# Phase-mixing kernel behind local attention: q and k of the last batch transposed by DMA, another order of the first loads, shallower load gates

## The chip, the cores and the metric

The kernel runs on one core of one Trainium2 chip. The metric is the device time of one execution in microseconds (us); less is better. The kernel before takes 171.01 us, the median of three runs (170.99 to 171.37).

## What is computed

Four batches, eight heads, 768 positions, head size 64; the model width is 8 x 64 = 512. First comes attention with a linear bias, where a position sees itself and the 95 positions before it (n_local = 96) and the first 8 positions (n_global = 8):

```python
scores = scale * q @ k.T + bias          # bias = -slope[h] * distance
scores = where(is_global | is_local, scores, -1e9)
a = exp(scores - max); a = a / (sum(a) + 1e-9)
x = (a @ v)  ->  [batch, 768, 512]
```

Then a block that mixes positions and channels:

```python
theta = x @ w_theta
zr, zi = x * cos(theta), x * sin(theta)
y = w_tok_r @ zr + w_tok_i @ zi          # over positions, per batch
u = x + y
out = u + max(u @ w_ch, 0)
```

## The kernel before

**Tiling.** The 768 positions are six tiles of 128. Two tiles make a "third", so a batch `b` has thirds `g` = 0, 1, 2. The 8 heads are four pairs `p`, since two heads of 64 fill 128 partitions.

**Operations and their names.** Each step is recorded by `add` under a name, and a list written out by hand, `ORDER`, says in which order the steps are issued. Each engine works off its own steps in that order, and waits where an operand or a buffer isn't ready. So the list sets the order on every engine, the DMA queues included. The names that matter here (digits are batch, third, and so on; a trailing `/DVE` or `/ACT` chooses the engine):

- `hw..`, `cast..`: q and k of the first third of batch 0 are loaded as float32 by plain DMAs on SP and ACT, and cast to bf16 (L293).
- `load<n>`: the n-th load on the queue of GpSimd (POOL), which casts from float32 to bf16 on the way: `load_qk` (L247), `load_v` (L261), `load_w` (L267), `load_w_tok` (L273). Their order is the order of the calls from L300 on; for the first loads the branch `ORD` chooses it.
- `gate<n>`: a copy of one element on POOL (L234) that reads what load n - depth has brought. It is issued just ahead of load n, so POOL can't issue load n until the earlier one has landed. The depth is 8 for batch 1 and `DEPTH` for batches 2 and 3.
- `t<b><g><i><u>`: the transpose of q (i = 0) or k (i = 1) of a third, to put the head size on partitions: eight 128x128 transposes on TensorE into PSUM (L425; L418 in the first third). `q...` and `k...` copy them out of PSUM (L439, L436). `kp` and `kg` (L384, L388) make a second copy of k whose first 8 columns are those of the global positions.
- `vpa`, `vpb` (L457, L460): the same second copy for v.
- `bi` (L490): a matmul that puts the bias into PSUM (batch 0 only). `s` (L499): scores. `x` (L526): exponential on ACT. `m` (L534): multiplication by `etab`, the exponential of the bias (L742), for batches 1 to 3. `v` (L556): values. `n` (L567, L569): the division by the sum.
- `xt` (L582 on TensorE with the copy `xc`; for batches 2 and 3 a DMA transpose on SP, L589): x transposed. `th` (L601): theta. `ts`, `tx`: loading of ACT's tables for sine and exponential (L733, L713). `cos`, `sin` (L610, L612), `z` (L622).
- `tw`, `twc` (L367, L372): the token weights transposed. `mx` (L644): the mixing over positions. `u` (L656). `ut`: u transposed, by DMA on SP (L676) or TensorE (L668, with the copy `uc`). `ch` (L688), `o` (L694), `st` (the store on SP, L704).

A name with `+n` asks for n fill matmuls on zeros ahead of its own (`fill`, L142 to 147), 128 columns wide into a bf16 tile (L145), else as wide as the tile (L147). The figures that are given to `add` for each engine (`{"DVE": 0.34}`) are estimates from which an order was once planned; when the kernel runs, only the first key of such an entry is used, as the engine where the list names none.

PSUM has two pools of four buffers, `pa` (scores, theta, values) and `pb` (the rest). A scores step takes two `pa` buffers, which the exponentials free; a theta takes one, which its sine frees.

Of the kernel before, what the change touches and what calls it, by code (L numbers as in the profile page):

```python
# [15 lines left out]
class Plan:  # L16
# [6 lines left out]
    def add(self, name, eng, fn, **_):  # L23
        op = self.ops[name] = SimpleNamespace(name=name, fn=fn, took=next(iter(eng)))
        return op
# [12 lines left out]
zero hw00 hw10 halfpi rel ones2 ones1 hw01 warm0 ones0 hw11 ones5 ones3 ones6 ones4 load1 tiny sid4 sid3 sid7  # L38
sid1 sid0 sid2 load2 sid5 sid6 ident far0 far1 load3 dtab0 dtab1 dtab2 load4 cast00/ACT dtab3 bi0000+1
cast10/DVE etab5 bi0001 t0000 load5 t0010 q000/ACT bi0010 bi0011 k000/DVE load6 etab7 kg000 cast01/DVE etab4  # L40
load7 kp000/DVE t0001+22 cast11/DVE etab1 s001 q001/DVE t0011 load8 etab0 s000 k001/DVE x0000 load9 kg001
x0001 kp001/DVE t0100+14 etab6 bi0020 load10 bi0021 q010/DVE x0010 t0110 x0011 s002 load11 k010/DVE etab2
bi0030 bi0031 s003 kp010/DVE x0020 load12 x0021 vpa00/DVE bi0100+2 x0030 kg010 vpb00/DVE bi0101+1 load13 x0031
s010 etab3 v000 v002 load14 v001 n000 x0100 bi0110 bi0111 vpa01/DVE s011 x0101 load15 vpb01/DVE bi0120 x0110
v003 n002 bi0121 load16 s012 x0111 n003 bi0130 load17 x0120 v010 n001 bi0131 s013 x0121 load18 n010 bi0200
x0130 v012 load19 v011 x0131 n012 t0200 gate20 t0210 n011 q020/ACT load20 v013 k020/DVE xt00 gate21 bi0201
kg020 xc00/ACT bi0210 kp020/DVE load21 bi0211 vpa02/DVE s020+1 n013 s021 gate22 x0200 vpb02/DVE load22 xt01+6
x0201 bi0220 x0210 xc01/DVE v020+1 bi0221 x0211 gate23 n020 bi0230 load23 s022 bi0231 x0220 s023 gate24 tw00
x0230 load24 th001 twc00/DVE x0231 gate25 x0221 v021 load25 v023 n021 ts0 tw10 gate26 v022 load26 twc10/DVE
th000 n023 gate27 tw11 n022 cos000 load27 th010 twc11/DVE sin000 xt02 gate28 cos001 z000 load28 tw01 sin001  # L50
th011 xc02/DVE gate29 cos010 z001 load29 th020 sin010 twc01/DVE gate30 cos011 load30 th021 z010 sin011 gate31
cos020 t1000 load31 z011 tw20 sin020 q100/DVE tw21 cos021 gate32 mx000 z020 load32 twc20/ACT twc21/DVE mx001
gate33 sin021 vpa10/DVE load33 tx1 vpb10/DVE t1010 z021 mx020 gate34 k100/DVE load34 mx002 kp100/DVE gate35
kg100 mx022 load35 u00 gate36 s100 load36 s101 ut00 x1000 mx021 gate37 x1010 uc00/DVE load37 x1001 tw31 x1011
u02 tw30 twc31/ACT gate38 s102 m100 load38 s103 t1100 x1020 m101 x1030 mx010 gate39 q110/DVE x1031 load39
x1021 v100 m103 mx012 twc30/ACT m102 gate40 load40 n100 tw40 v102 twc40/DVE mx011 gate41 n102 load41 t1110 u01
tw41 gate42 v103 k110/DVE load42 twc41/ACT ut01 ut02 v101 kg110 uc02/DVE ch00 uc01/ACT gate43 kp110/DVE load43
vpa11/DVE ch01 n103 gate44 load44 vpb11/DVE s110 n101 t1200 gate45 x1100 o00 load45 ch02 x1101 q120/DVE st00
t1210 gate46 o01 load46 s111 k120/DVE s112 st01 x1110 mx030 gate47 kp120/DVE x1120 load47 o02 mx032 x1121
kg120 gate48 x1111 m110 st02 mx031 load48 m111 s113 gate49 u03 s120 load49 x1130 tw50 m112 tw51 twc50/ACT v110  # L60
gate50 twc51/DVE xt10 load50 x1131 n110 mx040 vpa12/ACT xc10/DVE gate51 mx042 load51 m113 x1200 mx041
vpb12/DVE x1201 gate52 load52 m120 v111 mx050 n111 gate53 load53 u04 s121 v120 x1210 v113 gate54 n120 ut03
load54 x1211 mx052 n113 uc03/ACT gate55 m121 mx051 load55 vpa20/DVE s122 u05 gate56 s123 x1220 ch03 load56
vpb20/DVE x1221 ut04 x1230 gate57 o03 ut05 v121 load57 uc04/ACT v112 n121 th100 st03 uc05/ACT gate58 n112
x1231 load58 ch04 m122 ts1 m123 gate59 xt11 load59 v122 xc11/DVE cos100 v123 th101 gate60 n122 sin100 load60
n123 ch05 cos101 o04 gate61 sin101 xt12 load61 o05 st04 th110 xc12/ACT vpa21/DVE gate62 st05 z100 th111 load62
cos110 z101 sin110 th120 gate63 vpb21/DVE load63 cos111 z110 th121 sin111 gate64 cos120 load64 t2110 z111
sin120 t2010 k210/DVE gate65 cos121 t2200 load65 z120 mx100 k200/ACT kp210/DVE gate66 q220/DVE mx101 sin121
load66 kp200/DVE tx2 t2000 z121 gate67 mx120 kg210 load67 vpa22/DVE q200/DVE mx102 gate68 vpb22/DVE load68
kg200 mx110 u10 gate69 s200 load69 ut10 s201 mx111 x2000 x2001 gate70 x2010 mx121 load70 m200 x2011 v200 m201  # L70
gate71 mx112 load71 n200 s202 u11 gate72 s203 t2100 x2020 load72 x2021 mx122 ut11 q210/DVE x2030 gate73 x2031
m202 t2210 load73 u12 s210 k220/ACT s211 gate74 vpa30/DVE ut12 ch10 load74 vpb30/DVE x2100 kp220/DVE x2101
mx130 gate75 o10 load75 x2110 m210 s212 x2111 st10 mx131 gate76 m203 x2120 load76 m211 x2121 v210 mx132 n210
gate77 load77 m212 v201 s213 n201 ch11 gate78 x2130 load78 kg220 u13 x2131 v202 s220 n202 gate79 ut13 v203
load79 mx140 x2200 m213 x2201 n203 s221 gate80 load80 v212 vpa31/DVE x2210 xt20 mx142 m220 x2211 gate81 n212
s222 load81 v220 vpb31/DVE x2220 v213 n220 mx141 gate82 x2221 load82 n213 v211 m222 s223 ch12 n211 x2230 x2231
m221 v222 xt21 mx150 ts2 m223 v221 n222 v223 mx151 n221 n223 th200 o12 xt22 th201 o11 cos200 vpa32/DVE sin200
mx152 st11 u14 cos201 st12 vpb32/DVE ch13 sin201 ut14 u15 z200 th210 ut15 o13 th211 cos210 z201 sin210 st13
th221 cos211 z210 t3000 sin211 t3010 q300/DVE t3110 k300/DVE t3210 th220 k310/DVE k320/ACT kp300/DVE t3100
z211 cos220 mx200 kg300 q310/DVE sin220 mx201 cos221 kg310 kp310/DVE kg320 sin221 kp320/DVE t3200 z220 tx3  # L80
ch15 q320/DVE z221 s300 s301 mx220 x3000 o15 x3001 x3010 mx202 st15 m300 x3011 s302 m301 s303 mx222 u20 x3020
x3021 x3030 ut20 v300 m302 mx221 x3031 n300 v302 m303 ch14 n302 s310 o14 s311 x3100 mx210 u22 st14 x3110 v303
x3111 ut22 mx212 n303 x3101 m311 mx211 m310 v301 ch20 u21 n301 ut21 mx230 o20 s312 st20 s313 x3120 mx232 xt30
x3130 v310 x3121 ch22 n310 x3131 m312 s320 s321 o22 x3200 mx250 x3201 m313 st22 v311 x3210 mx231 n311 x3211
m320 s322 s323 u23 x3220 mx251 x3221 m321 ut23 v313 x3230 ch21 m322 x3231 n313 ts3 v312 v321 m323 mx240 n312
v320 o21 v322 xt31 mx241 n320 n321 v323 mx242 st21 n323 n322 th300 u24 xt32 mx252 cos300 sin300 th301 u25 ut24
z300 ch23 cos301 ut25 sin301 th310 o23 z301 th311 st23 cos310 sin310 mx300 cos311 z310 th320 sin311 z311 th321
cos320 sin320 mx301 cos321 z320 ch24 sin321 z321 mx310 o24 mx302 st24 mx311 u30 mx312 ut30 ch25 u31 mx320 ut31
o25 mx322 st25 mx321 ch30 u32 mx330 ut32 o30 mx331 st30 mx332 ch31 u33 mx340 ut33 o31 mx342 st31 mx341 ch32
u34 mx350 ut34 o32 mx351 st32 mx352 ch33 u35 ut35 o33 ch34 uc35/ACT st33 ch35 o34 ch351 o35 st34 o351 st35  # L90
st351
# [4 lines left out]
def kernel(  # L96
# [13 lines left out]
    nc = tc.nc  # L110
# [18 lines left out]
    add = plan.add  # L129
# [33 lines left out]
    TQ = ()  # L163
    TQ_AFTER = None
    DEPTH = 6
# [37 lines left out]
    add("dtab0", {"DVE": 0.34},  # L203
        lambda: nc.vector.tensor_tensor(dtab[:, 0:2], rel, far, op=ALU.add),
        reads=["far"], writes=["dtab"], prio=-6)
    add("dtab1", {"DVE": 0.11}, lambda: nc.vector.tensor_copy(out=dtab[:, 2], in_=dtab[:, 0]),
        reads=["dtab"], writes=["dtab"], prio=-6)
    add("dtab2", {"DVE": 0.14},
        lambda: nc.vector.tensor_scalar(dtab[0:NG, 0:2], dtab[0:NG, 0:2], float(NL), None, op0=ALU.min),
        reads=["dtab"], writes=["dtab"], prio=-6)  # L210
    add("dtab3", {"DVE": 0.14}, lambda: nc.vector.tensor_copy(out=dtab[:, 3:5], in_=dtab[:, 1:3]),
# [66 lines left out]
    def first(i, t):  # L278
# [18 lines left out]
        o = add(f"cast{i}{t}", {"DVE": 0.34, "ACT": 0.49}, cast, reads=[st], writes=[key, key + (i, t)],  # L297
# [10 lines left out]
    ORD = 2  # L308
# [66 lines left out]
    def twin(dst, mine, b, g, u0, n):  # L375
# [5 lines left out]

        def copy():
            d_ = tiles[dst][:, :, pr] if halves else tiles[dst][:, u0:u0 + n]
            vector[oc.took](out=d_[:, :, :, 1, NG:T], in_=d_[:, :, :, 0, NG:T])  # L384

        oc = add(f"kp{b}{g}{u0}", {"DVE": dve_t(512 * n, 4), "ACT": act_t(512 * n)}, copy, reads=mine, writes=[dst] + w2)
        add(f"kg{b}{g}{u0}", {"DVE": 0.1},
            lambda: nc.vector.tensor_copy(  # L388
                out=tiles[dst][:, td, kd, 1, 0:NG],
                in_=tiles["kk", b, 0][:, 0:1, kd, 0, 0:NG].to_broadcast([T, td.stop - td.start, kd.stop - kd.start, NG])),  # L390
            reads=mine + first_k, writes=[dst] + w2, boost=boost(b, 3))

    def trans_qk(b, g, i, ts):
# [404 lines left out]
```

The softmax here doesn't subtract the row's maximum and nothing guards it: scores larger than these inputs give would overflow.

## Time and profile before

| what | value |
|---|---|
| median of the runs | 171.01 us (170.99 to 171.37) |
| the profiled execution | 171.41 us |
| its span, first to last instruction | 169.6 us |
| TensorE (PE) busy | 162.1 us, 96% |
| VectorE (DVE) busy | 136.0 us, 80% |
| ScalarE (ACT) busy | 103.9 us, 61% |
| GpSimd (POOL) busy | 80.7 us, 48% |
| q and k transposes on PE (L425) | 176 |
| fill matmuls on PE (L145; L147) | 42; 6 |

The profile is that of one execution. Its time is the span and 1.8 us around it. "PE" is TensorE, whose matmuls overlap: the duration of one is longer than the step from one to the next, so costs are read from the chain of waits, where a run of matmuls is given as start, length and count. That chain is followed back from the last instruction, at each step to what released it. Views of waits give the total in us, the times and the longest. A window's row gives start and end, its length, then busy us and instructions of PE, the weight load of PE, DVE, ACT and POOL, the granted clock, the DMA share and GB/s. A row of DMA issues gives the transfer, the queue, the number, the size, and the median us from issue to landing.

### The profile page before, as it was taken

The numbers are of one execution on the slowest core, as the hardware profiler recorded it, in microseconds if no ns is written. First come the engines' busy times: TensorE is split into PE (matmuls) and PEld (weight loads), VectorE is DVE, ScalarE is ACT, GpSimd is POOL, SyncE is SP. The second block draws the span as 40 slices with busy tenths as digits, with TensorE's granted clock in tenths as the row PEclk, the third lists the DMA queues.
The fourth block names the chain that finished last, engine by engine and source line by source line (L and its number), as shares of the span: only waits on it lengthen the run. The fifth ranks groups of instructions, "written<-read, shape, count | busy, mean of one in ns | idle before, by whom it ended". The sixth has DMA issues, their size and how long they took to land.

```text
span 169.6 us, 4122 instructions
## 1 busy us (share of the span) xinstructions
PE 162.1 (96%) x1581; PEld 91.9 (54%) x1608; DVE 136.0 (80%) x316; ACT 103.9 (61%) x186; POOL 80.7 (48%) x150
## 2 busy tenths in 40 slices
PE   7999999999999999999999999999999999999990
PEld 2665756656655656565555554754545644444440
DVE  7888987896999999998699999898859965634442
ACT  3799989986454939994695666695448557200010
POOL 8998689969989989999950000000000000000000
PEclk9999999999999999999999999999999999999999
DMA  4999999999999999999999438303363373143334
GB/s 134 208 155 155 197 191 177 190 178 178 162 164 197 197 143 137 164 221 141 135 156 139 93 66 216 93 0 97 93 126 98 74 173 97 62 108 108 95 97 182
DMA packets 94820, 23.73 MB, mean 140 GB/s; under 512 B 86992, under 2 KB 91856, under 8 KB 94800
## 3 DMA queue, kind: packets, MB, share of 16 engines
q0 software_dynamic: 73504, 12.33, 96.4%
q1 hardware_dynamic: 20240, 10.62, 23.4%
q10 hardware_dynamic: 1056, 0.52, 1.2%
q8 instruction: 12, 0.20, 0.5%
q14 instruction: 8, 0.07, 0.1%
HBM read 25.69 MB, written 6.29 MB: 189 GB/s over the span
## 4 chain that ended last, share of the span: by engine, by line
PE 87%; DVE 6%; ACT 2%; issue 2%; DVEq 0%
PE pb L644 37%; PE pa L601 12%; PE pb L688 10%; PE pa L499 7%; PE pb L425 5%; PE pa L556 5%; PE pa L490 3%; PE pb L367 2%; PE pb L582 2%; PE pb L556 2%; ACT e L526 1%; PE pb L668 1%; DVE sid L215 1%; ACT etab L742 1%; DVE kk L384 1%
## 5 line engine op out<-in xcount | busy, mean ns | idle before, releaser
L644 PE MATMUL pb<-zri,w_tokT 128*128 128x512 bf16 x273 | 67.6, 379 | 1.0 <-issue 0.3
L526 ACT ACTIVATE e<-pa 128x512 bf16<-128x512 f32 (+1 forms) x96 | 47.2, 568 | 25.1 <-PE pa L499 25.0
L644 PEld LDWEIGHTS <-w_tokT 128*128 128x128 bf16 x288 | 25.9, 98 | 26.7
L656 DVE TENSOR_TENSOR u<-x,pb 128x512 bf16<-128x512 bf16 x24 | 16.4, 683 | 11.1 <-PE pb L644 11.1
L534 DVE TENSOR_TENSOR e<-e,etab 128x1024 bf16<-128x1024 bf16 (+1 forms) x36 | 22.3, 639 | 2.6 <-ACT e L526 2.4
L688 PE MATMUL pb<-w_ch_bf,uT 128*128 128x512 bf16 (+1 forms) x96 | 24.0, 371 | 0.2
L601 PE MATMUL pa<-w_theta_bf,xT 128*128 128x512 bf16 x90 | 22.5, 379 | 0.3
L610 ACT ACTIVATE cs<-pa,halfpi 128x512 bf16<-128x512 f32 x24 | 16.8, 700 | 7.9 <-PE pa L601 7.8
L261 POOL DMA_DIRECT2D vn<-in_v_dram x24 | 21.2, 892 | 0.6 <-DMA qk<-in_q_dram 0.4
L247 POOL DMA_DIRECT2D qk<-in_q_dram x22 | 19.6, 890 | 1.4 <-issue 0.7
L247 POOL DMA_DIRECT2D qk<-in_k_dram x22 | 19.3, 879 | 0.4 <-issue 0.3
L622 DVE TENSOR_TENSOR zri<-x,cs 128x1024 bf16<-128x1024 bf16 x24 | 16.4, 685 | 3.5 <-ACT cs L612 3.5
L556 PEld LDWEIGHTS <-e 128*128 128x128 bf16 x352 | 15.0, 98 | 5.8
L694 DVE SCALAR_TENSOR_TENSOR o<-pb,u 128x512 f32<-128x512 f32 (+1 forms) x25 | 16.3, 663 | 2.3 <-PE pb L688 2.3
L569 DVE TENSOR_TENSOR x<-pa,rec 128x256 bf16<-128x256 f32 x36 | 15.3, 425 | 1.2
L499 PE MATMUL pa<-qT,kk 64*128 64x128 bf16 x352 | 15.9, 218 | 0.3 <-DVE qT L436 0.2
L499 PEld LDWEIGHTS <-kk 64*128 64x128 bf16 x352 | 10.0, 94 | 10.8 <-issue 8.1
L612 ACT ACTIVATE cs<-pa 128x512 bf16<-128x512 f32 x24 | 14.7, 612 | 0.0
L672 ACT COPY uT<-pb 128x512 bf16<-128x512 bf16 x5 | 2.8, 589 | 18.8 <-PE pb L668 18.8
L601 PEld LDWEIGHTS <-xT 128*128 128x128 bf16 x96 | 9.0, 98 | 9.5 <-DVE xT L585 0.2
L688 PEld LDWEIGHTS <-uT 128*128 128x128 bf16 x100 | 8.9, 98 | 8.8 <-ACT uT L672 0.5
L425 PE MATMUL pb<-ident,qk 128*128 128x128 bf16 x176 | 12.5, 219 | 0.1
(76 smaller groups left out, 205.3 us busy)
## 6 DMA issues: line engine op xcount, KB each, us to landing
out_dram<-o SPq DMA_DIRECT2D x23, 256.0 KB, 2.5
vn<-in_v_dram POOLq DMA_DIRECT2D x24, 128.0 KB, 5.6
qk<-in_q_dram POOLq DMA_DIRECT2D x22, 128.0 KB, 5.7
qk<-in_k_dram POOLq DMA_DIRECT2D x22, 128.0 KB, 5.5
w_nat<-in_moe_w_tok_r_dram POOLq DMA_DIRECT2D x6, 192.0 KB, 7.9
w_nat<-in_moe_w_tok_i_dram POOLq DMA_DIRECT2D x6, 192.0 KB, 7.3
e<-in_k_dram ACTq DMA_DIRECT2D x2, 256.0 KB, 5.0
e<-in_q_dram SPq DMA_DIRECT2D x2, 256.0 KB, 4.3
```

The costliest lines, as they stand in the source:

```text
L247: nc.gpsimd.dma_start(out=tiles[key][:, i, t].rearrange("p (h d) -> p h d", d=D), in_=(q, k)[i][b, :, r0:r0 + T, :].rearrange("h p d -> p ...
L261: nc.gpsimd.dma_start(out=v_bufs[i][:, t, :, 0:D], in_=v[b, :, r0:r0 + T, :].rearrange("h p d -> p h d"))
L425: nc.tensor.transpose(p_[:, t - u0, p], tiles[key][:, i, t, p * T:(p + 1) * T], ident)
L499: nc.tensor.matmul(p_[hh][:, s], lhsT=tiles["kk", b, kg][R, kt, p, r, :], rhs=tiles["qT", b, g][R, qt, p, :], start=not biased, stop=not b ...
L526: nc.scalar.activation(tiles[ek][:, hh, 0:n], tiles[pb[hh]][:, 0:n], AF.Exp, scale=scale)
L534: nc.vector.tensor_mul(e_[:, :, 0:n], e_[:, :, 0:n], etab[:, 2 * p:2 * p + 2, s0:s0 + n])
L556: nc.tensor.matmul(o, lhsT=l_, rhs=r_, start=(i == 0), stop=(i == len(mms) - 1))
L601: nc.tensor.matmul(p_, lhsT=tiles["xT", b, g][:, p, t, :], rhs=w_theta_bf[:, p, :], start=(p == 0), stop=(p == NP - 1))
L610: nc.scalar.activation(tiles[ck][:, 0], tiles[ps], AF.Sin, bias=halfpi)
L622: nc.vector.tensor_mul(tiles[zk][:, t].rearrange("n i (p c) -> n i p c", p=NP), tiles["x", b, g][:, None, :, t, :].to_broadcast([T, 2, NP, ...
L644: nc.tensor.matmul(p_, lhsT=w_tokT[wi][:, 2 * g + t, tt * T:(tt + 1) * T], rhs=tiles["z", b, g][:, t, wi, :], start=(n == 1 and t == 0 and ...
L688: nc.tensor.matmul(p_, lhsT=tiles["uT", b, tt][:, p, :], rhs=w_ch_bf[:, p, i * w:(i + 1) * w], start=(p == 0), stop=(p == NP - 1))
```

## The change

The diff, with the list cut to two places:

```diff
-    TQ = ()
+    TQ = ((3, 0), (3, 1), (3, 2))
     TQ_AFTER = None
-    DEPTH = 6
+    DEPTH = 4
...
-    ORD = 2
+    ORD = 5
```

The branches of `ORD` that are concerned, unchanged in both kernels (`third(g)` is q and k of third g of batch 0):

```python
    elif ORD == 2:
        third(1), load_v(0, 0), load_v(0, 1), third(2), load_v(0, 2)
...
    elif ORD == 5:
        third(1), load_v(0, 0), third(2), load_v(0, 1), load_w("w_theta", w_theta_bf, moe_w_theta, 2.4), load_v(0, 2)
    if ORD < 3:
        load_w("w_theta", w_theta_bf, moe_w_theta, 2.4)
```

The branch of `trans_qk` that `TQ` selects, which was in the kernel before but not used:

```python
        if (b, g) in TQ:
            def go():
                ...
                nc.sync.dma_start_transpose(out=d_, in_=tiles[key][:, i].rearrange("n t c -> n (t c)"))
            add(f"t{b}{g}{i}{u0}", {"SP": 1.3}, go, ...)
            if i == 1:
                twin(dst, mine, b, g, u0, n)
            return
```

So for the three thirds of batch 3 six DMA transposes on SP's queue take the place of 48 transposes on TensorE and of the six copies out of PSUM; `kp` and `kg` stay.

The list is new as a whole; all engines get another order. The first lines, before and after, and the passage from batch 2 to batch 3:

```diff
-zero hw00 hw10 halfpi rel ones2 ones1 hw01 warm0 ones0 hw11 ones5 ones3 ones6 ones4 load1 tiny sid4 sid3 sid7
-sid1 sid0 sid2 load2 sid5 sid6 ident far0 far1 load3 dtab0 dtab1 dtab2 load4 cast00/ACT dtab3 bi0000+1
-cast10/DVE etab5 bi0001 t0000 load5 t0010 q000/ACT bi0010 bi0011 k000/DVE load6 etab7 kg000 cast01/DVE etab4
-load7 kp000/DVE t0001+22 cast11/DVE etab1 s001 q001/DVE t0011 load8 etab0 s000 k001/DVE x0000 load9 kg001
-x0001 kp001/DVE t0100+14 etab6 bi0020 load10 bi0021 q010/DVE x0010 t0110 x0011 s002 load11 k010/DVE etab2
...
-th221 cos211 z210 t3000 sin211 t3010 q300/DVE t3110 k300/DVE t3210 th220 k310/DVE k320/ACT kp300/DVE t3100
-z211 cos220 mx200 kg300 q310/DVE sin220 mx201 cos221 kg310 kp310/DVE kg320 sin221 kp320/DVE t3200 z220 tx3
-ch15 q320/DVE z221 s300 s301 mx220 x3000 o15 x3001 x3010 mx202 st15 m300 x3011 s302 m301 s303 mx222 u20 x3020
...
+zero hw00 hw10 ones3 rel ones1 ones2 hw01 warm0 ones0 hw11 ones4 ones5 tiny halfpi load1 ones6 far0 far1 dtab0
+load2 dtab1 dtab2 load3 dtab3 sid2 ident etab3 sid4 sid7 load4 sid5 sid1 cast00/DVE etab4 sid6 load5 sid0
+t0000+11 etab6 cast10/DVE bi0000 bi0001 q000/DVE etab0 t0010 load6 bi0010 k000/DVE cast01/ACT load7 kp000/DVE
+cast11/ACT t0001+18 kg000 sid3 etab2 q001/DVE s000+1 load8 t0011 x0000 bi0011 s001 k001/DVE x0001 load9 bi0020
+t0100 x0010 kg001 etab5 kp001/DVE bi0021 load10 bi0030 q010/DVE t0110 etab1 s002 load11 k010/DVE x0011 x0020
...
+mx150 m222 x2230 ut14 x2231 o11 v221 mx152 ts2 m223 ut13 v222 n221 v223 mx151 n222 t3000 n223 th201 o12 xt22
+th200 vpa32/DVE u15 th211 cos200 t3010 vpb32/DVE sin200 th210 cos201 z200 t3110 ch14 sin201 cos210 z201 ch13
+t3210 sin210 o14 cos211 mx210 o13 sin211 ut15 mx200 z210 z211 t3100 th220 th221 st12 cos220 st14 sin220
+kp300/DVE mx211 st13 kg300 cos221 z220 st11 s300 sin221 mx201 t3200 tx3 z221 s301 kg310 kp310/DVE mx212 x3000
+x3010 mx202 kg320 u21 x3001 x3011 kp320/DVE s302 ut21 u20 s303 ch15 x3020 m301 x3021 x3030 ut20 m300 mx220
```

The fills ("+n") are 22 and 14 ahead of `t0001` and `t0100`, 6 ahead of `xt01`, 1 to 2 ahead of `bi0000`, `bi0100`, `bi0101`, `s020` and `v020` before; after, they are 11 and 18 ahead of `t0000` and `t0001`, 1, 3 and 2 ahead of `s000`, `bi0031` and `bi0210`. The remaining lines of the diff change planned figures of `add` (such as `{"DVE": 0.34}` to `0.4`), which no running instruction uses.

## The prediction

> **What bounds the kernel now.** I read the page's first line, then who TensorE (PE) waits for, then busy time by stretch, then the chain of waits at the two places that the change touches.
>
> ```profile
> PE 162.1 (96%) x1581; PEld 91.9 (54%) x1608; DVE 136.0 (80%) x316; ACT 103.9 (61%) x186; POOL 80.7 (48%) x150
> ```
>
> ```profile
> PE pb L355 <- DVE zero L185: 1.2, 1, 1.2
> PE pb L644 <- issue: 0.3, 2, 0.2
> PE pa L147 <- ACT e L526: 0.2, 1, 0.2
> ```
>
> ```profile
> 0.00:15.00 15.00, 13.03 (x127) 7.58 (x129) 12.51 (x41) 10.61 (x20) 14.22 (x21) 1.00 1.74 165
> ...
> 35.00:105.00 70.00, 69.12 (x727) 40.26 (x739) 63.95 (x148) 47.74 (x86) 49.84 (x94) 1.00 1.75 157
> 105.00:115.00 10.00, 9.95 (x92) 6.00 (x92) 9.14 (x20) 8.22 (x15) 0.00 (x0) 1.00 0.22 58
> ```
>
> PE is busy for 96% of the span, its waits sum to about 2 us, and between 15 and 165 us it is idle for hardly 1%. The granted clock is 1.00 all the way. So past the first 15 us a microsecond of PE work taken away is a microsecond of time, as long as nothing else becomes late; an engine freed elsewhere gives nothing. In the first 15 us a part of "busy" is padding (next part), so there the chain decides, not the busy share.
>
> **Term 1: 48 transposes leave PE.** For batch 3, TQ turns six groups `t3..` of eight 128x128 transposes (L425) into DMA transposes on SP. The chain shows what they hold of PE, pipelined:
>
> ```profile
> 107.16 1.79 PE pb L425 x32
> 108.95 0.86 PE pa L601 x4
> 109.81 0.45 PE pb L425 x8
> ...
> 111.98 0.45 PE pb L425 x8
> ```
>
> 1.79 + 0.45 + 0.45 = **2.69 us** (0.056 us a transpose; the 219 ns of the group's row is one transpose's latency, not its pitch). They are links of the chain themselves, so nothing hides them. Their copies out of PSUM go too: five of 0.69 us on DVE and one of 1.01 us on ACT. These engines are not the bound; I count them at nothing.
>
> What is added is six transposes on SP, of 256 KB each like `xT<-x`:
>
> ```profile
> xT<-x SPq DMA_TRANSPOSE x6, 3.1
> ```
>
> The timeline has 1.24 us of SP for the issue of one, and 3.1 us from issue to landing. First need: `s300` reads k of the first third after `kp300` and `kg300` (0.40 + 0.17 us on DVE). On SP `t3010` stands behind `xt22`, which waits for the last norm `n223`. After `v223` ends, three norms take 3 x 0.55 = 1.65 us, `xt22` 1.25, then 3.1 to 3.4 for `t3010`, and 0.6 for the copies: 6.7 us. On PE, between `v223` and `s300` stand mx151, four thetas, ch14, ch13, mx210, mx200, th220, th221 and mx211: 12 x 0.865 = 10.4 us. Cover left: 3.7 us. Even the 5.4 us that two uT transposes took at 84 to 90 us, beside loads, would fit. `xt22` itself is wanted by th220, eight PE groups (7 us) after `v223`; 1.65 + up to 1.25 for the `t3000` ahead of it + 3.1 = 6.0. Cover 1 us. Behind the six on SP wait `ut15` and four stores; `ut15` is delayed by some 5 us and its user ch15 stands seven PE groups later; the stores' buffers are asked for later still. So the moved work is hidden; without that cover each late transpose would cost its whole lateness.
>
> What becomes tighter is ACT. Before, ACT had slack between the sines of batch 2 and the first exponentials of batch 3, given by these very transposes:
>
> ```profile
> 112.16 1.28 ACT L713 ACT_TABLE_LOAD   x1
> 113.45 0.20 ACT L713 ACTIVATE tiny<-tiny 1x1 f32<-1x1 f32 x1
> 113.60 1.64 ACT L526 ACTIVATE e<-pa 128x384 bf16<-128x384 f32 x4
> ```
>
> After: th220 and th221 stand together, so the second cosine and sine end 0.25 + 1.06 us after th221, the table takes 1.44, and x3001, third in ACT's order, ends 1.25 later: 4.0 us, and about 0.1 for semaphores. PE has in that time mx211, s300, mx201, s301, mx212, mx202 = 4 x 0.865 + 2 x 0.23 = 3.9 us before s302 wants the buffers. Stall 0.2 to 0.3 us; I take **+0.25**, bounds 0 (the thetas start a little earlier) and +1.0 (one more ACT copy of 1.01 us' size in between).
>
> The Trainium skill speaks against this part: "VectorE: DVE Perf Modes", section "Rules for kernel authors", says to transpose 128x128 on TensorE where a PSUM destination will do, and its section "The three transpose paths" gives 390 ns there against 1309 ns by DMA. The trace agrees on the order (0.056 us of PE pitch against 3.1/8 = 0.39 us by DMA). By that rule the part would gain nothing and the whole change about 0.7 us; but the rule prices a transpose alone and not an engine that is full.
>
> **Term 2: start-up and padding.** The new order also has fewer fill matmuls (the "+n"): transposes 42 -> 29, 13 x 0.056 = 0.73 us; wide ones 6 -> 6 with more of the 0.16 kind and fewer of 0.216, 0.17 us; together 0.90 us, of which 0.55 before the first values matmul. A fill only fills a wait: if the wait is there anyway, nothing is won. So the chain must be walked:
>
> ```profile
> 11.89 0.38 ACT e L526
> 12.27 0.62 ACT etab L742
> 12.89 0.39 ACT e L526
> ...
> 13.32 0.38 PE pa L147
> ```
>
> From 10.0 to 13.3 us ACT ends last: eight exponentials of the first third (0.41 each) with three etab (0.62) between. ACT began them at 10.0 since s000 ended there, behind DVE's casts and copies. After: DVE does the far/dtab chain first (from 1.65: 0.45 + 0.41 + 0.45 + 0.32 + 0.25 + 0.62, so dtab ends at 4.15 and not at 5.9; the next starts some 0.3 before that end, as it did before), then six of the sid and ident (0.23 each), cast00 at 5.3, two sid, cast10 to 6.65, q000 and k000 (0.65 each) to 8.0, kp000 and kg000 to 8.6 to 9.0. So s000 ends at 8.9 to 9.4 and ACT starts 0.6 to 1.1 earlier; its five etab and two casts of before that (from 4.15: 5 x 0.65 + 2 x 0.6) end at 8.6 and are no obstacle. DVE's further chain (q001, k001, kp, kg, q010, k010, kp, kg, then vpa00, vpb00) ends at 14.0 to 14.6 against 14.77 before. I take **-0.6**, bounds -1.0 and +0.2 (the slow rows of the same copies: vpa00 took 0.84 and not 0.43). Later pads: 0.35 us fewer; before had no PE wait there, so I take **-0.3**, bounds -0.35 and 0.
>
> Moved loads, in POOL's queue at 0.87 us a place and some 6.9 us to landing: q, k of the last third come two places earlier; v of the middle third four places later, at 17.7 to 18.6 us, and its users moved behind s021 (about 21 us); w_theta two places earlier, at some 20 to 21 us, wanted by th001 at about 23.3; v of the last third at some 22, wanted by v020 at 25. Each has over 1 us of cover: nothing. If the cover of v went, PE would wait by the lateness.
>
> **Term 3: gates four deep, from load 47 on.** A gate on POOL waits until the load four places earlier has landed; behind it on POOL stand all later loads. Six deep, the 36 loads took 40.2 us, 1.12 us each (0.87 issue, 0.18 gate copy, few waits). Four deep the pace is at least (landing + 0.2) / 4. The landing depends on what is under way; two short stretches (47 to 50 us, 50 to 56 us beside stores):
>
> ```profile
> qk<-in_q_dram POOLq DMA_DIRECT2D x2, 128.0 KB, 4.5
> ```
> ```profile
> qk<-in_q_dram POOLq DMA_DIRECT2D x2, 128.0 KB, 6.7
> ```
>
> With 4.5 us the pace is 1.18 and the last v lands at 91.5 + 36 x 0.06 = 94; with the window's median of 5.0 it is 1.30 and 98. Its first user is this DVE copy, which stands in DVE's order ahead of u15 and will come some 3 us sooner:
>
> ```profile
> 102.35 0.43 DVE L457 COPY vp<-vn 128x1040 bf16<-128x1040 bf16 x1
> ```
>
> 99.5 at the earliest: hidden, **0**, bounds 0 (fewer transfers in the way of uT, at 5.4 us there, which nobody waits for) and +4 (second rival).
>
> **Sum.** -2.69 + 0.25 - 0.6 - 0.3 = **-3.3 us** against the profiled execution's 171.41 (span 169.6 and 1.8 around it): span about 166.3, time 168.1. The runs' median is 171.01, 0.4 below that execution, so 167.7.
>
> **Rivals.**
> 1. Waits take the place of fills and transposes: start-up gives nothing (the DVE chain ends at 14.8 as before, 0), later pads -0.2, and the ACT hinge costs 0.8. -2.69 - 0.2 + 0.8 = -2.1: 168.9. For it: three of four terms are small differences of queues. Against: PE waited 0.2 us for ACT in the whole of before.
> 2. Slower: the gate. If landing stays at 5.7 us or more with four under way, the pace is 1.48, the last v lands at 91.5 + 36 x 0.36 = 104.4, 4.9 us after vpa32's turn; DVE stands there, behind it u15 and the z of batch 2, and PE follows when the 1 us or so of groups that don't need them are done: some +4 (an estimate): 171.01 - 3.3 + 4.0 = 171.7, more with longer landings. It decides from a pace of 1.34, a landing of 5.2 us. For it: 5.0 to 5.7 medians. Against: 4.5 in the stretch with only four under way.
> 3. The transposes don't leave the chain: DMA transposes in a row of five on SP land late enough (by over 3.7 us at s300) to eat the 2.69 us; with -0.6 left of the rest: 170.4. Against: rows of three uT and xT in a row at 136 to 140 us landed in 2.4 to 3.3 us.
>
> **How the numbers follow.** Forecast 0.58 (all better bounds, -2.69 - 1.0 - 0.35 = -4.0, give 167.0, less 0.3 by which runs differ: 166.7; start-up at +0.2 gives 168.5), rival 1 0.20, rival 2 0.13, rival 3 0.09. Range 166.7 to 169.7: the forecast, rival 1 with 0.8 us above it for more such waits, about 8 in 10 with it; 2 in 10 lie with rivals 2 and 3 above. A measurement tells about 0.3% (0.5 us) from no change. Faster: forecast, rival 1 and half of rival 3 (the price of its late landings is open by as much), 0.82; within: the other half and the mild end of rival 2, 0.07; slower: the rest of rival 2, 0.11.
>
> **What would show it.** L425 with 128 matmuls instead of 176, still no PE wait over 0.5 us between 15 and 160; `qT<-qk` and `kk<-qk` on SP landing in 3.0 to 3.6 us; first values matmul at 14.0 to 14.6; a PE wait for ACT of 0.2 to 0.3 us at the first exponentials of batch 3; last v load landed by 98 us. It would be wrong if DVE waits for `vn` from DMA near 100 us, PE waits for `kk`, or PE's idle time in the first 15 us grows by over 0.5 us.

## Result and profile after

The changed kernel takes **179.93 us**, the median of four runs (178.94 to 181.16), against 171.19 for the kernel before in the same job (170.99 to 171.66): a ratio of 1.051, 95% interval 1.044 to 1.058. It is slower by some 8.7 us; the forecast was 167.7 us, with a range of 166.7 to 169.7. The profiled execution took 179.51 us, its span is 177.7. Line numbers after the change are one less than before (L643 was L644). Where the executions of a kernel scatter, the ratio is taken from its undisturbed ones alone, so it needn't be the ratio of the medians.

The page's first line and its row of granted clock, slices of 4.44 us:

```profile
PE 163.3 (92%) x1523; PEld 89.1 (50%) x1547; DVE 132.2 (74%) x315; ACT 101.0 (57%) x181; POOL 83.0 (47%) x150
...
PEclk9999999999999999999999999957999999999998
```

TensorE (PE) has 58 matmul records fewer (48 of them the transposes) and 1.2 us more busy time, in a span 8.1 us longer. From 115.5 us on, two slices show a clock of about 0.5 and 0.7. Busy time by stretch (columns: window, its length, then PE, PEld, DVE, ACT, POOL busy, granted clock, DMA share, GB/s) puts the loss in one place:

```profile
0.00:15.00 15.00, 12.38 (x118) 7.53 (x119) 12.47 (x41) 11.18 (x21) 14.22 (x21) 1.00 1.79 164
35.00:105.00 70.00, 68.81 (x723) 39.47 (x734) 62.06 (x147) 45.49 (x81) 51.96 (x95) 1.00 1.74 149
...
110.00:130.00 20.00, 14.42 (x119) 6.38 (x120) 10.62 (x27) 9.38 (x19) 0.00 (x0) 0.83 0.53 133
```

Who waits there, first PE's waits, then those of VectorE (DVE):

```profile
PE pb L643 <- DVE zri L621: 5.4, 1, 5.4
...
PE pa L146 <- ACT e L525: 0.6, 2, 0.4
PE pb L555 <- DVE vp L459: 0.5, 1, 0.5
```
```profile
DVE o L693 <- DMA out_dram<-o: 7.3, 1, 7.3
...
DVE vp L456 <- DMA vn<-in_v_dram: 1.8, 3, 1.1
```

PE waits 5.4 us at once for z, and DVE, which makes z, waits 7.3 us for a *store to HBM*. The chain of waits shows why the store is late. Columns: start, us, what.

```profile
108.60 0.89 SPq L401
...
109.65 1.26 SPq L401
...
111.01 1.22 SPq L675
...
112.28 1.30 SPq L401
...
113.64 2.33 DMA out_dram<-o
...
116.06 0.69 DVE o L693
116.75 0.61 DVE zri L621
...
117.40 1.86 PE pb L643 x4
119.27 0.43 PE pa L498 x6
119.70 1.82 PE pb L643 x4
```

Read it upwards. PE's matmul at 117.40 waits for `z210`, the first z behind the output step `o13` on DVE (L693, 116.06). `o13` needs a buffer of the pool `o`, which has three; they hold `o11`, `o12` and `o14`, whose stores are all still queued on SP. The first of these is that of `o12`. DVE is idle from 108.7 us on. `o12` was computed by 104.3 us, but its store `st12` was issued at 113.64: on SP it stands behind `t3010`, `t3110`, `t3210`, `ut15` and `t3100`, of 1.2 to 1.3 us each. It landed 2.33 us later, and only then could DVE go on. When PE starts again, four matmuls take 1.86 and 1.82 us instead of 0.86: the granted clock falls to 0.50 at 115.36 us, 3.3 us into PE's idle time, and is 1.00 again from 122.19 on. PE thus works for 4.8 us at half the clock, which costs another 2 us. The Trainium skill, "TensorE: Matmul & The Clock Gate", section "Part 1: The HAM clock gate", states a halved clock after an idle window of about 3.4 us. The trace agrees: 3.3 us here, 3.6 us in the run e2 below.

The loads: the last load of v was issued at 98.91 and landed at 104.44 (before: 86.22 and 91.49). Load 47, the first that is gated four deep, already waits for a load that is longer under way (timeline of POOL, in brackets the idle time before):

```profile
46.75 0.88 POOL L260 DMA_DIRECT2D vn<-in_v_dram  x1
49.08 0.18 POOL L233 COPY scrap<-w_nat 1x1 bf16<-1x1 bf16 x1 [1.45 <-DMA w_nat<-in_moe_w_tok_r_dram]
49.62 0.87 POOL L246 DMA_DIRECT2D qk<-in_q_dram  x1 [0.36 <-DVE x L568]
```

From there the last 36 loads follow one another at (98.91 - 49.62) / 35 = 1.41 us, against (86.22 - 47.55) / 35 = 1.10 before (the 1.12 of the prediction is the whole stretch by 36).

### The profile page after: what moved, and what is told of

It reads as the page before. It is cut to its first block, busy times and chain, and to the rows that moved or that the text cites. A ratio compares the mean times of both kernels' runs of the same rounds, so it can differ in the third digit from the quotient of the medians.

```text
span 177.7 us, 4022 instructions
## 1 busy us (share of the span) xinstructions
PE 163.3 (92%) x1523; PEld 89.1 (50%) x1547; DVE 132.2 (74%) x315; ACT 101.0 (57%) x181; POOL 83.0 (47%) x150
## 4 chain that ended last, share of the span: by engine, by line
PE 53%; DMA 19%; DVE 9%; issue 6%; POOL 6%; SPq 3%; ACT 1%; DVEq 0%; POOLq 0%; ACTq 0%
PE pb L643 21%; DMA qk<-in_q_dram 9%; PE pb L687 8%; PE pa L600 8%; DMA vn<-in_v_dram 7%; PE pa L498 4%; DMA uT<-u 3%; POOL scrap L233 2%; POOL qk L246 2%; PE pb L354 2%; PE pa L489 2%; SPq L401 2%; PE pb L555 2%; POOL vn L260 2%; ACT e L525 1%
## 5 line engine op out<-in xcount | busy, mean ns | idle before, releaser
L643 PE MATMUL pb<-zri,w_tokT 128*128 128x512 bf16 x276 | 69.3, 387 | 6.0 <-DVE zri L621 5.4
L643 PEld LDWEIGHTS <-w_tokT 128*128 128x128 bf16 x288 | 26.5, 98 | 34.4 <-issue 7.4
L693 DVE SCALAR_TENSOR_TENSOR o<-pb,u 128x512 f32<-128x512 f32 (+1 forms) x25 | 16.4, 664 | 13.0 <-DMA out_dram<-o 7.3
L260 POOL DMA_DIRECT2D vn<-in_v_dram x24 | 22.1, 925 | 2.0 <-issue 1.8
L498 PE MATMUL pa<-qT,kk 64*128 64x128 bf16 x352 | 17.7, 221 | 1.2 <-DVE x L568 0.5
L555 PEld LDWEIGHTS <-e 128*128 128x128 bf16 x352 | 14.1, 98 | 5.5 <-issue 0.6
L555 PE MATMUL pa<-vn,e 128*128 128x65 bf16 x144 | 12.3, 194 | 0.0
L671 ACT COPY uT<-pb 128x512 bf16<-128x512 bf16 x2 | 1.2, 585 | 18.9 <-PE pb L667 18.8
```

Source lines behind the costliest of these rows:

```text
L260: nc.gpsimd.dma_start(out=v_bufs[i][:, t, :, 0:D], in_=v[b, :, r0:r0 + T, :].rearrange("h p d -> p h d"))
L498: nc.tensor.matmul(p_[hh][:, s], lhsT=tiles["kk", b, kg][R, kt, p, r, :], rhs=tiles["qT", b, g][R, qt, p, :], start=not biased, stop=not b ...
L555: nc.tensor.matmul(o, lhsT=l_, rhs=r_, start=(i == 0), stop=(i == len(mms) - 1))
L643: nc.tensor.matmul(p_, lhsT=w_tokT[wi][:, 2 * g + t, tt * T:(tt + 1) * T], rhs=tiles["z", b, g][:, t, wi, :], start=(n == 1 and t == 0 and ...
L693: nc.vector.scalar_tensor_tensor(o_[:, c], in0=tiles["ch", b, tt, i], scalar=0.0, in1=tiles[uk][:, c], op0=ALU.max, op1=ALU.add)
```

## Experiments

Theory **A**: `o13` waits for the store `st12`, which the DMA transposes on SP hold up; that is the main loss. Theory **B**: the gates four deep make the loads late, DVE falls behind, and the wait for the store only follows. Three runs take one cause or both out of the changed kernel; a fourth puts the gates alone into the kernel before.

### e1_store_first: the store ahead of the transposes

```diff
-... vpa32/DVE u15 th211 cos200 t3010 ... t3100 th220 th221 st12 cos220 ...
+... vpa32/DVE u15 th211 cos200 st12 t3010 ... t3100 th220 th221 cos220 ...
```


> The changed kernel with one step moved in the list: the store st12 stands on SP ahead of the transposes t3010, t3110, t3210, ut15 and t3100 instead of behind them. Theory A (the DVE step o13 needs the output buffer that st12 reads, and st12 stood behind five transposes): the 7.3 us wait of DVE at L693 for out_dram<-o goes, and PE's 5.4 us wait with it, and the half clock after it; 172 to 174 us against 179.9. Rival B (late loads hold DVE at the copy of v and everything behind it): the wait turns into one for vn or for the transposes, 176 us or more.

Measured: 174.35 us, ratio 1.018 (1.013 to 1.024), 0.35 above what theory A expected. Its waits, of PE and of DVE, and one row of DVE's timeline:

```profile
PE pa L498 <- DVE x L568: 2.7, 2, 2.1
```
```profile
DVE vp L456 <- DMA vn<-in_v_dram: 4.0, 2, 2.7
...
DVE o L693 <- DMA out_dram<-o: 1.1, 1, 1.1
```
```profile
98.30 0.44 DVE L456 COPY vp<-vn 128x1040 bf16<-128x1040 bf16 x1 [2.73 <-DMA vn<-in_v_dram]
```

One store moved ahead of five steps on SP gives back 5.6 us; DVE's wait for a store falls from 7.3 to 1.1 us, and PE no longer waits for z. What is left to see is the late v. The row is `vpa31`, the copy of v of the middle third; `vpa30` waited 1.25 us, and `vpa32`, for the last v, not at all.

### e2_depth6: the changed kernel with gates six deep

```diff
-    DEPTH = 4
+    DEPTH = 6
```


> The changed kernel with gates six deep again and all else as it is. Theory A: the last v lands near 92 us and not 104, DVE's waits for vn go, but st12 still stands behind the transposes: DVE still waits 5 us or more at L693; 176.5 to 178.5 us. Rival B (late loads are the cause, the store's wait only follows from them): 169 to 172 us, no wait over 2 us at L693.

Measured: 178.15 us, 1.041 (1.036 to 1.046): 1.8 us better, no more, as theory A expected. The stall is still there, while DVE waits for no load of v:

```profile
PE pb L643 <- DVE zri L621: 4.3, 1, 4.3
```
```profile
DVE o L693 <- DMA out_dram<-o: 6.3, 1, 6.3
```

So B falls as the main cause.

### e3_both: both edits

> The changed kernel with both: st12 ahead of the transposes and gates six deep. Theories A and B: the two losses are gone, 169 to 171.5 us; what is left against the forecast of 167.7 is then the start-up, which the trace after shows 0.65 us later at the second values step in place of 0.6 earlier. If it stays above 173, a third cause is at work in the new order.

Measured: 171.84 us, 1.004 (1.002 to 1.006), 0.3 above what A expected, and 4.1 above the forecast of 167.7. The waits that are new against before are small:

```profile
PE pb L687 <- DMA uT<-u: 1.1, 3, 0.5
PE pa L146 <- ACT e L525: 0.6, 2, 0.4
PE pb L555 <- DVE vp L459: 0.5, 1, 0.5
PE pa L498 <- DVE qT L435: 0.5, 1, 0.5
```

### e4_before_depth4: the kernel before with gates four deep

> The kernel before with gates four deep and nothing else. Theory A: the last loads land some 10 us later, near 102, and DVE waits for vn by 1 to 2 us near 102 us; 171.5 to 173.5 us. Rival B: late loads are the main loss, 175 us or more. If the kernel before has enough slack, 171 (no change).

Measured: 173.7 us (171.32 to 175.39), ratio 1.010 (1.006 to 1.014). By the ratio 1.6 us are lost, by the median of all ten runs 2.7, and its executions scatter over 4 us where those of before scatter over 0.8. It shows the wait that rival 2 of the prediction named, 1.55 us at `vpa31` and 1.06 at `vpa32`:

```profile
DVE vp L457 <- DMA vn<-in_v_dram: 2.6, 2, 1.5
```

### e6_o4: a fourth buffer, the order as changed

This tests whether the buffer, and not the store's place, makes `o13` wait.

```diff
-    bufs = dict(..., uT=3, o=3, w_nat=7, pa=4, pb=4)
+    bufs = dict(..., uT=3, o=4, w_nat=6, pa=4, pb=4)
```


> The changed kernel with its order as it is, four deep, but a fourth buffer for o (and one buffer fewer for the natural token weights, to make room). The stores stay behind the transposes on SP. Theory A (the step o13 waits for the store st12 only since it needs that store's buffer): the DVE wait for out_dram of 7.3 us goes, PE's wait of 5.4 us for zri goes, time 173 to 175.5 us, as with the store moved. Rival C (what helped in that run was another place of the store in SP's queue, for instance the transposes' own time): still 177.5 us or more, with PE waiting over 3 us at L643.

Measured: 174.05 us, 1.016 (1.014 to 1.018), as e1. SP still issues the stores late, and no step of DVE or PE waits for one any more:

```profile
108.53 4.07 SPq L401 DMA_TRANSPOSE kk<-qk  x3
112.69 1.23 SPq L675 DMA_TRANSPOSE uT<-u  x1
113.98 1.30 SPq L401 DMA_TRANSPOSE qT<-qk  x1
115.33 2.03 SPq L703 DMA_DIRECT2D out_dram<-o  x4
```

Two different cures have one result: A holds, and the link is the buffer.

### e5_before_tq: the kernel before, with the DMA transposes alone

The second question is the 4.1 us that e3 leaves. Here only `TQ` is set; the names of PE's copies leave the list, and the DMA transposes stand where SP has time, none of them ahead of a store that is soon wanted.

```diff
-    TQ = ()
+    TQ = ((3, 0), (3, 1), (3, 2))
-... xt20 mx142 ... xt21 mx150 ... o13 th211 ... st13 th221 cos211 ...
+... xt20 t3010 t3000 mx142 ... xt21 t3110 mx150 ... o13 th211 ... st13 t3210 t3100 t3200 th221 cos211 ...
-... mx201 cos221 kg310 kp310/DVE kg320 sin221 kp320/DVE t3200 z220 ... st15 m300 ...
+... mx201 cos221 kg310 kp310/DVE sin221 z220 ... st15 kg320 kp320/DVE m300 ...
```


> The order of before, six deep, its old start-up, with only one part of the change: q and k of batch 3 by DMA transposes, and these placed on SP ahead of the stores whose buffers are soon wanted (k of the first third right behind xt20, k of the second behind xt21, the last three behind st13). Theory A (the 2.69 us that the PE transposes hold of the chain are really saved when SP's queue delays nobody; what was lost in the changed kernel was lost in its order and gates): 168.0 to 169.2 us, ratio 0.982 to 0.989, no PE wait over 0.6 us between 15 and 160 us, L425 with 128 matmuls. Rival R (six DMA transposes on SP bring a wait wherever they stand, or PE waits for kk or qT): 170.0 to 172 us with a PE or DVE wait of 1.5 us or more for a DMA.

Measured: **168.79 us**, 0.987 (0.986 to 0.989): 2.3 us faster than before, and the fastest of all kernels here. Its page, and its exponentials at the turn to batch 3:

```profile
PE 159.5 (95%) x1534; PEld 89.4 (54%) x1560; DVE 132.7 (79%) x311; ACT 102.8 (62%) x185; POOL 83.5 (50%) x150
```
```profile
109.95 1.28 ACT L712 ACT_TABLE_LOAD   x1
111.24 0.20 ACT L712 ACTIVATE tiny<-tiny 1x1 f32<-1x1 f32 x1
111.35 3.11 ACT L525 ACTIVATE e<-pa 128x384 bf16<-128x384 f32 x8
```

PE's busy time falls by 2.6 us and the profiled span by 2.6 (the profiled execution of before was 0.4 slower than the median). PE has no new wait, and DVE none of over 0.2 us for a DMA. So the rival falls which says that transposes on SP cost a wait wherever they stand.

### e8_newstart: e5 with the change's start-up

The order of the first 30 us with its fewer fills, and the order of the first loads, from the changed kernel:

```diff
-    ORD = 2
+    ORD = 5
```


> The kernel with only the DMA transposes (order of before), plus the change's start-up: the order of the first 30 us and the order of the first loads are those of the changed kernel, with its fewer fill matmuls; the rest stays. The forecast priced this part at -0.6 and up to -0.3: by it 167.2 to 168.2 us where the kernel without it gives 168.5. Theory S (the fills that were dropped come back as waits on the copies of v and on the exponentials): within 0.4 us of the kernel without the new start-up. Rival S2 (the new start-up loses, as TensorE's lag of 1.2 us at 35 us in the changed kernel says): 0.6 to 1.5 us more than without it.

Measured: 169.32 us, 0.990 (0.988 to 0.992). It is 0.5 above e5, between the two expectations; the two intervals touch, so the start-up loses between nothing and about 1 us, and doesn't gain the 0.9 that was forecast. The timelines of DVE and PE show the place:

```profile
13.10 0.97 DVE L456 COPY vp<-vn 128x1040 bf16<-128x1040 bf16 x1
14.10 0.83 DVE L459 COPY vp<-vn 8x1040 bf16<-8x1040 bf16 x1
```
```profile
14.22 0.24 PE L555 MATMUL pb<-vn,e 128*128 128x65 bf16 x2
14.99 0.19 PE L555 MATMUL pb<-vp,e 128*128 128x65 bf16 x1 [0.53 <-DVE vp L459]
```

The lines are those of the changed kernel; e8 has the same wait, 0.54 us. The first matmul of the values comes earlier (14.22), and the next one stands still for the copy `vpb00`.

### e9, e10, e11, e12: the changed order up to, or from, a point

Each has the DMA transposes and the gates six deep, as e5 has, and takes the changed order for another stretch: e9 up to the end of batch 1 (58 us), e10 and e11 up to the end of batch 2 (110 us, with `st12` first), e12 for batch 3 alone.

> The changed kernel's order up to the end of batch 1's attention (to about 58 us), six deep, and from there the order of before with the DMA transposes as in the run that did them alone. It tells where the 2.4 us are lost that lie between the new start-up alone (169.3) and the new order throughout, six deep, with the store moved (171.8). Theory P (the loss is spread over the order, a few tenths wherever scores are cut into more runs on TensorE and uT is wanted sooner): 169.6 to 170.4 us. Rival Q (it lies in batch 2 and 3 alone, at the waits for uT and the first exponentials): 169.0 to 169.5 us.

Measured: 169.86 us, 0.993 (0.991 to 0.996), 0.5 above e8, as theory P has it, though the two intervals overlap.

> The changed kernel's order up to the end of batch 2 (to about 110 us), with the store ahead of the transposes and six deep, and from there the order of before. Theory P: 170.3 to 171.2 us, PE waits of about 1 us in all for uT at ch10, ch11. Rival Q: 170.2 to 171 us as well if the loss sits in batch 2, and 169.0 to 169.6 us if it sits in batch 3; the two runs together tell the three apart.

Measured: 172.15 us, 1.007 (1.004 to 1.010), above both expectations. The seam made a wait of its own: the order of before wants `ch15` early, and `ut15` stands on SP behind three transposes (timeline of PE):

```profile
112.56 1.04 PE L687 MATMUL pb<-w_ch_bf,uT 128*128 128x512 bf16 x4 [2.26 <-DMA uT<-u]
```

So this run says nothing yet of batch 2, and e11 mends the seam:

```diff
-... st12 t3010 vpb32/DVE ... z200 t3110 ... t3210 ... ut15 ...
+... st12 t3010 vpb32/DVE ... z200 ut15 t3110 ... t3210 ...
```


> The run with the changed order to the end of batch 2, once more, with one place on SP changed: uT of u15 ahead of the transposes of k of the second and last third, not behind them. There TensorE waited 2.3 us for this uT at ch15, since the order of before wants ch15 early. Theory W (that wait was the whole loss of that run, and batch 2's order costs nothing): 169.6 to 170.2 us, no wait for uT over 0.3 us near 112 us. Rival (batch 2's order itself costs, by scores in more and shorter runs on TensorE): 171 to 172 us, wait or no wait.

Measured: 170.27 us, 0.994 (0.991 to 0.996). That wait is gone and 1.9 us with it, a little less than theory W expected. DVE now waits 1.9 us for `kk` from DMA, since k comes later on SP, but PE doesn't. Batch 2's order costs 0.4 by the medians (e11 - e9) and next to nothing by the ratios (0.994 and 0.993).

> The run with only the DMA transposes (order of before, 168.8 us) to the end of batch 2, and the changed kernel's order for batch 3 behind it. If the remaining loss of some 2 us sits in batch 3's order (ch24 waiting for uT, scores waiting for exponentials, scores cut into more runs): 169.8 to 170.8 us, with PE waits of 0.5 us or more after 113 us. If batch 3's order costs nothing: 168.5 to 169.1 us.

Measured: 169.63 us, 0.990 (0.987 to 0.992). It lies between the two expectations, 0.8 above e5. PE has no new wait of 0.5 us in batch 3; its busy time is 0.4 longer (159.9 against 159.5).

### The sum

These are differences of medians, each from two kernels that differ in one part or one stretch of the order, from jobs in which the kernel before took 171.01 to 171.19. DMA transposes -2.3 (e5); new start-up +0.5 (e8 - e5); rest of batch 0 and batch 1 +0.5 (e9 - e8); batch 2 +0.4 (e11 - e9); batch 3 +0.8 (e12 - e5). That makes 171.1 - 2.3 + 2.2 = 171.0 for e3, which took 171.84; the 0.8 between fits the 1.1 us of waits for uT that e3 has and e9, e11 and e12 have not, though no run isolates them. Apart from the DMA transposes, each of these is hardly larger than the intervals of the runs it comes from. Gates four deep: +2.5 (e1 - e3). The store: +5.6 (changed kernel - e1), or 6.3 with gates six deep (e2 - e3). The last two steps lead from e3 to the changed kernel, so they close the sum of 179.9 by themselves and don't test it.

## Why the prediction was wrong

**The step that failed** is in term 1: "the stores' buffers are asked for later still. So the moved work is hidden". It asked who needs what the transposes bring, and who needs `ut15`; all of that was in time (`kk` and `qT` landed in 3.1 to 3.4 us, `qT` once in 4.5, and PE never waited for them in the changed kernel). It did not ask, store by store, who needs the *buffer* that the store empties. `o` has three buffers, and with `o11`, `o12` and `o14` done, `o13` needs one whose store is still queued. The numbers were at hand: the stores of before land after 2.5 us (median row), and with five issues of 1.25 us that puts the buffer over 8 us behind the start of `t3010`; behind `o13` on DVE stood the z that PE needs at once. What the runs showed in place of "hidden": DVE waited 7.3 us for the store of `o12`, PE 5.4 us for z, and the price was 5.6 us.

**Term 1's gain** was right in its mechanism and close in size: -2.69 forecast, 2.3 measured in e5, by the profiled span 2.6. The rule that the prediction set against this part, by which it would gain nothing, did not decide here, where PE was busy for 96% of the span. The +0.25 for ACT at the first exponentials could not be told in the changed kernel, where the stall covers it; e3 shows no wait of PE for ACT there, and e5's eight exponentials run without a gap.

**Term 3**, gates four deep, was taken as 0 with +4 as its other end; it cost 1.6 to 2.7 us. The first step that was off is the pace: (landing + 0.2) / 4 was a lower bound and was used as the value. The 36 loads landed in 4.8 us on average, so the formula gives 1.25, and 1.41 was measured: a round of four took some 0.8 us more than a landing, not 0.2. No run splits these 0.8 us. Load 47 also started 2.1 us later than before (49.62 against 47.55), which was not counted. The second step is the cover: the term looked at the last v alone, whose copy `vpa32` it put at 99.5 us. With loads in time (e3) that copy came at 104.0, later than the 102.35 of before, and in the changed kernel it waited only 0.22 us. The copies for the earlier loads of v waited: `vpa30` 0.51 us and `vpa31` 1.09, in e1 1.25 and 2.73.

Rival 2 had the mechanism, DVE waiting for late v, and was given 0.13. That its landing of the last v came true (104.4 forecast, 104.44 measured) is partly luck: its pace of 1.48 was too slow, and the late start of load 47 was not in it. It placed the wait at `vpa32` too.

**Term 2**, start-up -0.6 and fills -0.3, came out as about +0.5. The front end was read rightly: exponentials began 0.6 us earlier (9.38 against 10.01) and the first values matmul at 14.22 (14.82 before). But the stage ends with the copies of v, and DVE's chain to them, put at 14.0 to 14.6 us, ended at 14.93 (14.77 before). Of the lead of 0.6 us only 0.09 was left where `vpa00` began (13.10 against 13.19), and the two copies of v took 0.97 and 0.83 us where those of before took 0.84 and 0.71. The slow copy was named as the bad end of the range and not taken. The time of the dropped fills came back as waits: 0.53 us for `vpb00`, 0.6 for ACT (0.2 before), 0.5 for qT (0.2 before).

**What no term held**: the changed order of batches 1 to 3 was priced by its fills alone. It cost 1.7 us in the three pieces of the sum, and mostly not as waits. One part can be estimated. In the changed kernel scores go to PE in 39 separate runs instead of 33; by the chain of before, eight scores matmuls alone hold PE for 0.33 us and sixteen in one run for 0.55, so an extra run costs about 0.1 us. One of the six extra runs belongs to the start-up, and the three pieces hold four of them (two in e9, none in e11, two in e12): 0.4 of the 1.7 us. No run tests this estimate, and the rest is unsettled.

**The rivals.** Rival 1 (waits take the place of fills) happened at the start-up. Rival 2 is term 3. Rival 3, that late transposes eat their gain, did not happen: in e5 the gain is there. The mechanism that decided was none of them.

## What to carry to other kernels

When instructions are put into an in-order queue, walk everything behind them to what it *releases* as well as to what it delivers: a store that nobody reads still holds a buffer, and when all buffers of the pool wait for stores, the next producer stops, with its whole engine behind it. Put such stores ahead of the transfers whose users are far away, or add a buffer; here the first cure was worth 5.6 us (6.3 with gates six deep), the second 5.9. When a change bundles a part with a clean price (-2.3) and a rewritten order, build the part alone in the old order first.

## What the runs showed that was not expected

- A long stall of PE cost twice here: the stalls of 5.4 us and, in e2, of 4.3 us were each followed by matmuls at half the granted clock (four in 1.86 us, not 0.86), for 4.8 and 6.0 us; the stall of 2.26 us in e10 was not (the matmuls behind it took 1.04 by the row, as elsewhere).
- Gates four deep gained less in landing than they lost in pace. In the changed order the last 36 loads landed in 4.8 us on average, six deep (e2) in 5.7, while the step from load to load was 1.41 against 1.19 us; in the order of before it was 4.9 (e4) against 5.1 us, and 1.42 against 1.10.
- In e9 the three DMA transposes of uT that were issued at 81 to 87 us, beside loads, landed in 5.8 to 6.3 us, and the last five, issued after 146 us with no loads under way, in 2.4 to 2.5. Those between took 2.4 to 4.3 us.
